# Attention with mixed heads and a gated feed-forward: moving four of a group's six products with v inside and across units

## The chip, the cores and the metric

The kernel runs on one core of a Trainium2 chip. The metric is the device time of one execution in microseconds. "Before" was timed in three runs, and one further execution was profiled.

## What is computed

For 4 batches, 12 heads, 448 positions and head size 64, scores are mixed over the heads before and after the softmax; the result, laid out as 1792 tokens of width 768, goes through a bilinear feed-forward of width 1536. The random inputs q, k and w_pre are multiplied by 8.

```python
scores = scale * np.matmul(q, k.transpose(0, 1, 3, 2))
scores = np.einsum('bhij,hg->bgij', scores, w_pre)
scores = scores - np.max(scores, axis=-1, keepdims=True)
attn = np.exp(scores)
attn = attn / (np.sum(attn, axis=-1, keepdims=True) + 1e-09)
attn = np.einsum('bhij,hg->bgij', attn, w_post)
x = np.matmul(attn, v)          # then tokens x (heads * head size)
out = ((x @ w_a) * (x @ w_b)) @ w_out
```

## The kernel before

The attention is cut into 92 units of at most 20 query positions (23 per batch: 6, 6, 6 and 5, from chunks of 120, 120, 120 and 88 positions). The main loop over `s` (L898 to L933) is software-pipelined; one pass does a piece of several units, and the order of the calls in it is the order of the instructions on each engine. TensorE executes in one pass:

- `premix(s)` (L345, tile `mp`): 8 matmul records that mix the heads of the scores of unit `s`, in 60x64 quadrants. `mp` has three buffers of one bank and a unit takes two, so the second block of a unit reuses the buffer of the first block of the unit before it, and waits for that block's exponential.
- one `qk` (L281, tile `pst`): raw scores for a later chunk. `pst` has one buffer (`bufs=1`), so the next `qk` waits until this one is copied out, by VectorE (L306) or by ScalarE (L308). With `OWN = 3` the copy of product `i` of a chunk is ScalarE's where `i % 3 == 0`. From unit 11 to unit 82 there is one `qk` in each unit, with `i = (s + 7) % 6`; from unit 83 on there is none, and pieces of the feed-forward are prepared instead.
- one `av(a, p)` (L429, tile `xp`): the `p`-th of the six products with v of group `a`. It is 16 matmuls that use all 128 rows and 64 columns of the array (128x64). A group is the 6 (or 5) units of one chunk, and its width is 120 (or 88). After the third and the sixth product VectorE copies `xp` out (L438), and a later DMA stores it (L439).
- `postmix(s - 1)` (L391, tile `pp`): 56 matmuls in 60x64 quadrants. It reads the exponentials of unit `s - 1` and `kr` (L373), and it writes two banks that must first have been emptied of unit `s - 2` by `evac_p` (L408, two ScalarE copies).

ScalarE's order in a pass is `evac_p(s - 2)`, two exponentials (L358) each with a read of its sum, and the `pst` copy where it is ScalarE's. VectorE's is two maxima (L355), in 18 units three copies that reorder k (L242 to L244, one set per unit, units 10 to 15, 34 to 39 and 58 to 63), the `pst` copy where it is VectorE's, the `xp` copy if there is one, and three small instructions for the norm (L368, L369, L373).

The products with v stand in the dictionary `items` with the `qk`: L460 to L464 place product `p` of group `a` at unit `u0 + n + AV_AT[p]`, one per unit. A 5-unit group uses `AV_SHORT`, which puts its first two products into one unit. The last group's six products run after the loop. A planner for loads (L466 on) reads only `av_at`, the unit of each product.

```python
    AV_AT = (1, 2, 3, 4, 5, 6)
    AV_SHORT = (2, 2, 3, 4, 5, 6)
            for it in items.get(s, ()):           # qk first, then av
```

Of the kernel before, what the change touches and what calls it, by code (L numbers as in the profile page):

```python
# [22 lines left out]
def talking_heads_bilinear_kernel(  # L23
# [21 lines left out]
    GU = 6  # L45
# [40 lines left out]
    for b in range(B):  # L86
        t0 = 0
        while t0 < S:
            n = min(CHUNK, S - t0)
# [115 lines left out]
    def load_v(b, i):  # L205
        g, i = divmod(i, V_PIECES // 2)
        to, of = vt[b % 2][g], v[b, g]
        if i < 3:
            heads = slice(2 * i, 2 * i + 2)
            nc.sync.dma_start(out=to[:C, heads], in_=of[:C, heads])  # L210
        elif i < 5:
            heads = slice(3 * (i - 3), 3 * (i - 3) + 3)
            nc.sync.dma_start(out=to[C:P, heads, :R - 1], in_=of[C:, heads, :R - 1])
        elif i == 5:
            for j in range(R - 1):
                nc.sync.dma_start(out=to[P:, :, j], in_=of[C + Y * j:C + Y * j + Y, :, R - 1])
        else:
            nc.sync.dma_start(out=to[C:, :, R - 1], in_=of[:C, :, R - 1])
# [91 lines left out]
    def halves(n):  # L310
        return [(o, min(QH, n - o)) for o in range(0, n, QH)]

    def gather(u):
        c, o, n = units[u]
        sbt[u] = [sb_p.tile([128, S], F32, tag=f"sb{e}", name="sb") for e in range(2)]
        for i, (t, m) in enumerate(halves(n)):
            r = 64 * (i // 2)
            nb = chunks[c][2] // QB
            k_ = (o + t) // QB
            r0 = 64 * (t % QB // QH)  # L320
            if k_ < nb:
                rows = st[c][r0:r0 + QH * nb].rearrange("(i k) h s -> k i h s", k=nb)[k_]
            else:
                rows = st[c][r0 + QH * nb:r0 + QH * nb + m]
            (nc.sync if ALONE <= u <= AH and i % 2 else nc.gpsimd).dma_start(out=sbt[u][i % 2][r:r + m * H], in_=rows)  # L325

    def blocks_of(u):
        n = units[u][2]
        return [(u, j, min(QB, n - QB * j)) for j in range(2) if n > QB * j]
# [4 lines left out]
    def premix(u):  # L334
        n = units[u][2]
        tiles = sbt.pop(u)
        for k_ in blocks_of(u):
            mt[k_[:2]] = ps.tile([128, 512], F32, tag="m", name="mp", bufs=3)[:, :S]
        for i in (0, 2, 1, 3):
            if i >= len(halves(n)):  # L340
                continue
            m = halves(n)[i][1] * H
            r, col = 64 * (i // 2), 64 * (i % 2)
            M = 64 if n == QU or i == 0 else m
            nc.tensor.matmul(mt[u, i // 2][col:col + M], lhsT=wp[r:r + m, :M], rhs=tiles[i % 2][r:r + m])  # L345

    def smax(k_):
        u, j, n = k_
        m = rows_of(n)
        mp = mt.pop((u, j))  # L350
        if j == 0:
            rss[u] = w_p.tile([128, 2], F32, tag="rs", name="rs", bufs=12)
        nm = w_p.tile([128, 1], F32, tag="nm", name="nm", bufs=16)
        a = w_p.tile([128, S], F32, tag="an", name="a", bufs=AB)
        nc.vector.tensor_reduce(nm[:m], mp[:m], axis=AXX, op=ALU.max, negate=True)  # L355
        if j == 0:
            pace(2 * u, nm)
        nc.scalar.activation(a[:m], mp[:m], ACTF.Exp, bias=nm[:m], scale=1.0, accum_out=rss[u][:m, j:j + 1])  # L358
        at[u, j] = a

    def norm(u):
        rs = rss.pop(u)
        rc = w_p.tile([128, 2], F32, tag="rc", name="rc", bufs=8)
        kr = w_p.tile([128, 2, H * QH], F32, tag="kr", name="kr", bufs=3)
        ms = [rows_of(n) for _, _, n in blocks_of(u)]
        for j0, j1 in ([(0, len(ms))] if ms[0] == ms[-1] else [(0, 1), (1, 2)]):
            m = ms[j0]
            nc.vector.tensor_scalar(rs[:m, j0:j1], rs[:m, j0:j1], 1e-9, None, op0=ALU.add)  # L368
            nc.vector.reciprocal(rc[:m, j0:j1], rs[:m, j0:j1])  # L369
            if j0 == 0:  # L370
                pace(2 * u + 1, rc[:, :1])
            shape = [m, j1 - j0, H * QH]
            nc.vector.tensor_tensor(  # L373
                kr[:m, j0:j1],
                kf[:m].rearrange("p h t -> p (h t)").unsqueeze(1).to_broadcast(shape),
                rc[:m, j0:j1].unsqueeze(2).to_broadcast(shape),
                op=ALU.mult,
            )
        krs[u] = kr.rearrange("p j (h t) -> p j h t", h=H)

    def postmix(u):
        kr = krs.pop(u)
        blocks = blocks_of(u)
        todo = [[(j, r, e) for r in range(R - 1) for e in range(2)] + [(j, R - 1, j)] for j in range(len(blocks))]
        if len(blocks) == 2:
            todo[1] = todo[1][-1:] + todo[1][:-1]
        for j, r, e in [x for t in todo for x in t]:
            x = C * (r + R * e if r < R - 1 else r)
            for i, (_, m) in enumerate(halves(blocks[j][2])):
                rows = slice(64 * i, 64 * i + m * H)  # L390
                nc.tensor.matmul(  # L391
                    pp_t[i][C * e:C * e + C, H * r:H * r + H, j, :m],
                    lhsT=at[u, j][rows, x:x + C],
                    rhs=kr[rows, j, :, :m],
                )
        for j in range(len(blocks)):
            at.pop((u, j))

    def evac_p(u):
        a = group_of[u]  # L400
        n = units[u][2]
        o = (u - groups[a][1]) * QU
        if a not in ptt:
            ptt[a] = big.tile([128, R, H, AVC], F32, tag="pt", name="pt")
        to = ptt[a].rearrange("p r h t -> p (r h) t")
        for i in range(2):
            if n == QU:
                nc.scalar.copy(to[:, :, o + QB * i:o + QB * i + QB], pp_t[i].rearrange("p x j t -> p x (j t)"))  # L408
                continue
            for j, (_, _, m) in enumerate(blocks_of(u)):  # L410
                hs = halves(m)
                if i < len(hs):
                    t0, k = hs[i]
                    t0 += o + QB * j
                    nc.scalar.copy(to[:, :, t0:t0 + k], pp_t[i][:, :, j, :k])
# [23 lines left out]
            later(lambda: nc.sync.dma_start(out=xd[b][:, 3 * g:3 * g + 3, t0:t0 + n], in_=xs[:, :, :n]), 1)  # L439

    items, late, between, after, ready = {}, {}, {}, {}, {}
    starts = [u for u in range(NU) if units[u][1] == 0] + [NU]
    qk_at = {}
    last_prep = starts[NC - 1] - AH - 1
# [12 lines left out]
    av_at = {}  # L457
    for a in range(NA):
        b, u0, n = groups[a]
        for p in range(H // 2):  # L460
            av_at[a, p] = u0 + n + (AV_AT if n == GU else AV_SHORT)[p]
            if a < NA - 1:
                items.setdefault(av_at[a, p], []).append((av, a, p))

    def plan_loads():
        per_b = NC // B  # L466
# [45 lines left out]
    def open_moe():  # L512
        short.close()
        mo["w"] = ctx.enter_context(tc.tile_pool(name="mw", bufs=2))
        mo["x"] = ctx.enter_context(tc.tile_pool(name="mx", bufs=1))
        mo["x"].tile([128, PAD_X], F32, tag="pad", name="pad")
# [335 lines left out]
    with tc.manual_schedule():  # L852
# [45 lines left out]
        for s in range(NU + 2):  # L898
            now[0] = s
            if s == last_prep + 1:  # L900
                open_moe()
            while nxt_g <= min(s + AH, NU - 1) and ready.get(units[nxt_g][0], -1) < s:
                gather(nxt_g)
                nxt_g += 1
            if 0 <= s - V_FIRST < V_PIECES - V_EARLY:
                load_v(0, V_EARLY + s - V_FIRST)
            for fn in todo_at.pop(s, ()):
                fn()
            if s < NU:
                premix(s)  # L910
            if 2 <= s <= NU:
                evac_p(s - 2)
            if s < NU:
                for k_ in blocks_of(s):
                    smax(k_)
            for it in between.get(s, ()):
                it[0](*it[1:])
            for it in items.get(s, ()):
                if it[0] is qk:
                    it += (it[2] % OWN if s not in late else 1,)  # L920
                it[0](*it[1:])
            if s < NU:
                norm(s)
            if 0 <= s - 1 < NU:
                postmix(s - 1)
            for it in late.get(s, ()):
                qk(*it[1:], 0)
            for it in after.get(s, ()):
                it[0](*it[1:])
            for fn in at_end.pop(s, ()):  # L930
                fn()
            if s == NU:
                evac_p(NU - 1)  # L933
# [142 lines left out]
```

## Time and profile before

| what | us |
|---|---|
| median of 3 runs (lowest, highest) | 862.87 (862.2, 865.9) |
| the profiled execution's own time | 862.92 |
| span of the profiled execution, first to last instruction | 861.2 |
| TensorE busy in the span | 837.9 |

In a row of the timeline the columns are the start in us from the start of the span, the duration in us from the first start to the last end, the engine (PE is the matmuls of TensorE, PEld its weight loads, DVE VectorE, ACT ScalarE), the line of the kernel, the operation, output and input tile with their shapes, and the number of instructions merged into the row. In square brackets stands the idle time of the engine before it and what ended that. Matmuls overlap in the array, so the length of a TensorE block is read from its start to the start of the next block.

### The profile page before, as it was taken

How to read it: one execution, taken by the hardware profiler on the slowest of the kernel's cores; microseconds unless marked ns; L12 is line 12 of the kernel's file. 1: busy time of each engine (PE TensorE's matmuls, PEld its weight loads, DVE VectorE, ACT ScalarE, POOL GpSimd, SP SyncE). 2: the span in 40 equal slices, each digit the busy share in tenths (PEclk: the TensorE clock that was granted, in tenths of full speed). 3: DMA queues.
4: the chain of work that ended last, by engine and by line, in shares of the span. 5: the costliest groups of instructions: out<-in, count | busy, mean ns of one | idle time of the engine just before them, and what ended most of it. 6: DMA issues, size and time to landing. Idle time of an engine off the chain costs nothing.

```text
span 861.2 us, 26229 instructions
## 1 busy us (share of the span) xinstructions
PE 837.9 (97%) x10612; PEld 672.9 (78%) x10612; DVE 499.4 (58%) x989; ACT 414.6 (48%) x864; POOL 479.5 (56%) x595
## 2 busy tenths in 40 slices
PE   6999999999999989999999999999999999999998
PEld 3356566566656556799999999999999998999997
DVE  4688677777787767465433433363445244655761
ACT  3577677667777767644323332322233145333330
POOL 6777777677767856036446533678666743222220
PEclk9899999999999999999999999999999999999999
DMA  8777886787979974674543634566565488654551
GB/s 199 177 210 176 188 199 196 181 199 187 205 178 213 202 194 112 194 228 164 190 146 135 217 135 152 193 216 248 198 227 191 151 319 309 216 213 186 200 198 65
DMA packets 105306, 165.90 MB, mean 193 GB/s; under 512 B 50014, under 2 KB 81114, under 8 KB 105186
## 3 DMA queue, kind: packets, MB, share of 16 engines
q1 hardware_dynamic: 76738, 126.11, 46.3%
q0 software_dynamic: 28448, 38.11, 18.6%
q8 instruction: 84, 1.38, 0.7%
q14 instruction: 36, 0.29, 0.1%
HBM read 84.16 MB, written 41.29 MB: 146 GB/s over the span
## 4 chain that ended last, share of the span: by engine, by line
PE 84%; DMA 5%; DVE 3%; issue 2%; POOL 2%; ACT 2%; SPq 1%; DVEq 0%; POOLq 0%; ACTq 0%
PE xp L429 9%; PE pp L391 8%; PE mp L345 7%; PE pst L281 7%; PE pa L639 6%; PE pa L641 6%; PE pb L639 6%; PE pa L640 6%; PE pb L641 6%; PE pb L640 6%; PE po L760 5%; PE po L759 5%; PE po L758 5%; DMA sb<-s 2%; DMA hr<-hd 1%
## 5 line engine op out<-in xcount | busy, mean ns | idle before, releaser
L325 POOL DMA_DIRECT2D sb<-s x354 | 205.2, 592 | 63.8 <-PE mp L345 28.6
L358 ACT ACTIVATE a<-mp,nm 124x448 f32<-124x448 f32 x180 | 112.8, 632 | 58.8 <-DVE nm L355 58.7
L355 DVE TENSOR_REDUCE nm<-mp 124x1 f32<-124x448 f32 x180 | 104.2, 619 | 55.7 <-PE mp L345 55.1
L661 DVE TENSOR_TENSOR hf<-pb,sa 128x448 f32<-128x448 f32 x47 | 29.3, 624 | 164.5 <-PE pb L641 157.7
L429 PEld LDWEIGHTS xp<-pt,v 128*64 128x64 f32 x1536 | 74.1, 136 | 63.5 <-issue 43.5
L645 ACT COPY sa<-pa 128x448 f32<-128x448 f32 x47 | 25.2, 536 | 176.9 <-PE pa L641 176.9
L408 ACT COPY pt<-pp 128x480 f32<-128x480 f32 x176 | 91.3, 576 | 34.0 <-PE pp L391 33.0
L345 PE MATMUL mp<-sb,wp 60*64 60x448 f32 x720 | 98.6, 550 | 4.5 <-DMA sb<-s 2.8
L391 PE MATMUL pp<-kr,a 60*64 60x60 f32 x5040 | 97.6, 222 | 4.8 <-issue 4.2
L640 PE MATMUL pb<-xhl,wh 128*128 128x448 f32 x282 | 102.2, 362 | 0.0
L639 PE MATMUL pb<-xhl,wh 128*128 128x448 f32 x282 | 102.2, 362 | 0.0
L641 PE MATMUL pb<-xhl,wl 128*128 128x448 f32 x282 | 102.2, 362 | 0.0
L391 PEld LDWEIGHTS pp<-kr,a 60*64 60x64 f32 x5040 | 85.1, 134 | 21.4 <-issue 9.6
L281 PE MATMUL pst<-k,q 64*64 64x448 f32 (+1 forms) x728 | 92.7, 545 | 4.6 <-ACT s L308 2.6
L429 PE MATMUL xp<-pt,v 128*64 128x120 f32 (+1 forms) x1536 | 93.4, 265 | 2.4 <-ACT a L358 0.8
L641 PE MATMUL pa<-xhl,wl 128*128 128x448 f32 x264 | 95.7, 362 | 0.0
L639 PE MATMUL pa<-xhl,wh 128*128 128x448 f32 x264 | 95.7, 362 | 0.0
L640 PE MATMUL pa<-xhl,wh 128*128 128x448 f32 x264 | 95.7, 362 | 0.0
L630 POOL TENSOR_TENSOR wl<-v,wh 128x768 fp32r<-128x768 f32 x21 | 38.9, 1851 | 98.6 <-ACT wh L629 98.6
L760 PE MATMUL po<-hhl,wl 128*128 128x448 f32 x252 | 91.5, 363 | 0.8 <-POOL wl L630 0.8
L758 PE MATMUL po<-hhl,wh 128*128 128x448 f32 x252 | 91.3, 362 | 0.0
L759 PE MATMUL po<-hhl,wh 128*128 128x448 f32 x252 | 91.3, 362 | 0.0
(117 smaller groups left out, 1430.3 us busy)
## 6 DMA issues: line engine op xcount, KB each, us to landing
sb<-s POOLq DMA_DIRECT2D x350, 105.0 KB, 5.0
hhl<-hd SPq DMA_DIRECT2D x42, 448.0 KB
v<-in_w_ab_dram SPq DMA_DIRECT2D x22, 768.0 KB
hd<-hf SPq DMA_DIRECT2D x48, 224.0 KB
v<-in_w_out_dram SPq DMA_DIRECT2D x12, 768.0 KB
wod<-cw SPq DMA_DIRECT2D x21, 384.0 KB
v<-wod SPq DMA_DIRECT2D x21, 384.0 KB
xhl<-xd SPq DMA_DIRECT2D x24, 224.0 KB
```

What stands on the lines that cost most here:

```text
L281: nc.tensor.matmul(out[64 * e:64 * e + cols.stop - cols.start], lhsT=qt[c, i // QG][rows, i % QG, cols], rhs=kt[b, i][rows],)
L325: (nc.sync if ALONE <= u <= AH and i % 2 else nc.gpsimd).dma_start(out=sbt[u][i % 2][r:r + m * H], in_=rows)
L345: nc.tensor.matmul(mt[u, i // 2][col:col + M], lhsT=wp[r:r + m, :M], rhs=tiles[i % 2][r:r + m])
L358: nc.scalar.activation(a[:m], mp[:m], ACTF.Exp, bias=nm[:m], scale=1.0, accum_out=rss[u][:m, j:j + 1])
L391: nc.tensor.matmul(pp_t[i][C * e:C * e + C, H * r:H * r + H, j, :m], lhsT=at[u, j][rows, x:x + C], rhs=kr[rows, j, :, :m],)
L429: nc.tensor.matmul(xp[64 * e:64 * e + 64, p % 3, :n], lhsT=vt[b % 2][g][:, h % G, r], rhs=ptt[a][:, r, h, :n], start=(r == 0), stop=(r == ...
L639: nc.tensor.matmul(o, lhsT=hh[:, off + k], rhs=x[:, 0, k], start=first, stop=False)
L640: nc.tensor.matmul(o, lhsT=hh[:, off + k], rhs=x[:, 1, k], start=False, stop=False)
L641: nc.tensor.matmul(o, lhsT=ll[:, off + k], rhs=x[:, 0, k], start=False, stop=last)
L758: nc.tensor.matmul(po, lhsT=hh[:, k], rhs=t[:, 0, k], start=(k == 0), stop=False)
L759: nc.tensor.matmul(po, lhsT=hh[:, k], rhs=t[:, 1, k], start=False, stop=False)
L760: nc.tensor.matmul(po, lhsT=ll[:, k], rhs=t[:, 0, k], start=False, stop=(k == KH2 - 1))
```

## The change

For a group of 6 units the second product with v (`p` = 1) leaves its place between `qk` and `postmix` and comes behind `postmix` in the same pass; the third (`p` = 2) comes ahead of `premix` in its pass, which is the next one. The fifth and the sixth go the same way. So in TensorE's order products 2 and 3 stand next to each other across the boundary of two passes, as do 5 and 6. The first and the fourth stay. In the 5-unit groups only the fifth and the sixth move. The unit of each product is unchanged. The `xp` copy after the third and the sixth product moves with them, ahead of the maxima of its pass; its store (one pass later) and all loads keep their places.

```diff
     items, late, between, after, ready = {}, {}, {}, {}, {}
+    ahead, behind = {}, {}
+    AV_WHEN = (items, behind, ahead) * 2
...
             if a < NA - 1:
-                items.setdefault(av_at[a, p], []).append((av, a, p))
+                when = AV_WHEN[p] if n == GU or p > 2 else items
+                when.setdefault(av_at[a, p], []).append((av, a, p))
...
             for fn in todo_at.pop(s, ()):
                 fn()
+            for it in ahead.get(s, ()):
+                it[0](*it[1:])
             if s < NU:
                 premix(s)
...
             if 0 <= s - 1 < NU:
                 postmix(s - 1)
+            for it in behind.get(s, ()):
+                it[0](*it[1:])
             for it in late.get(s, ()):
```

## Rows read from the trace of the kernel before

**Rows 1.** The page: busy time of the engines; the chain that ended last.

```profile
PE 837.9 (97%) x10612; PEld 672.9 (78%) x10612; DVE 499.4 (58%) x989; ACT 414.6 (48%) x864; POOL 479.5 (56%) x595
...
PE 84%; DMA 5%; DVE 3%; issue 2%; POOL 2%; ACT 2%; SPq 1%; DVEq 0%; POOLq 0%; ACTq 0%
```

**Rows 2.** Timeline of TensorE's matmuls, unit 32 and the start of unit 33.

```profile
137.91 0.94 PE L345 MATMUL mp<-sb,wp 60*64 60x448 f32 x8
138.66 0.93 PE L281 MATMUL pst<-k,q 64*64 64x448 f32 x8
139.53 1.04 PE L429 MATMUL xp<-pt,v 128*64 128x120 f32 x16
140.50 1.04 PE L391 MATMUL pp<-kr,a 60*64 60x60 f32 x56
141.36 0.94 PE L345 MATMUL mp<-sb,wp 60*64 60x448 f32 x8
```

**Rows 3.** Timeline of TensorE's matmuls, a unit with two products and one with one.

```profile
113.95 1.44 PE L429 MATMUL xp<-pt,v 128*64 128x88 f32 x32
115.32 1.04 PE L391 MATMUL pp<-kr,a 60*64 60x60 f32 x56
...
117.80 0.83 PE L429 MATMUL xp<-pt,v 128*64 128x88 f32 x16
118.56 0.63 PE L391 MATMUL pp<-kr,a 60*64 60x60 f32 x28
```

**Rows 4.** Timeline of TensorE's matmuls, early units that have no product with v.

```profile
28.15 0.98 PE L281 MATMUL pst<-k,q 64*64 64x448 f32 x8
28.95 0.99 PE L391 MATMUL pp<-kr,a 60*64 60x60 f32 x56
29.77 1.36 PE L345 MATMUL mp<-sb,wp 60*64 60x448 f32 x8
31.01 0.98 PE L281 MATMUL pst<-k,q 64*64 64x448 f32 x8
...
34.22 0.98 PE L281 MATMUL pst<-k,q 64*64 64x448 f32 x8 [0.44 <-ACT s L308]
```

**Rows 5.** Timeline of TensorE's matmuls near the end, a `postmix` before a product.

```profile
356.55 1.04 PE L391 MATMUL pp<-kr,a 60*64 60x60 f32 x56
357.52 1.04 PE L429 MATMUL xp<-pt,v 128*64 128x120 f32 x16
```

**Rows 6.** Timeline of ScalarE and of the weight loads around those early units.

```profile
29.37 0.63 ACT L358 ACTIVATE a<-mp,nm 124x448 f32<-124x448 f32 x1 [2.47 <-DVE nm L355]
...
30.15 0.20 PEld L345 LDWEIGHTS mp<-sb,wp 60*64 60x64 f32 x6 [0.24 <-ACT a L358]
...
33.27 0.90 ACT L308 COPY s<-pst 124x896 f32<-124x896 f32 x1
```

**Rows 7.** Timeline of ScalarE in unit 32, where the `pst` copy is ScalarE's.

```profile
139.67 0.63 ACT L358 ACTIVATE a<-mp,nm 124x448 f32<-124x448 f32 x1 [0.50 <-DVE nm L355]
...
140.90 0.90 ACT L308 COPY s<-pst 107x896 f32<-107x896 f32 x1
```

**Rows 8.** Timeline of a unit whose `pst` copy is VectorE's: its `premix`, maxima, copy.

```profile
215.75 0.94 PE L345 MATMUL mp<-sb,wp 60*64 60x448 f32 x8
...
216.78 1.16 DVE L355 TENSOR_REDUCE nm<-mp 124x1 f32<-124x448 f32 x2 [1.12 <-PE mp L345]
217.86 1.08 DVE L306 COPY s<-pst 107x896 f32<-107x896 f32 x1
```

**Rows 9.** Timeline of unit 12, which reorders k: its `premix` and its `pst` copy.

```profile
66.28 0.94 PE L345 MATMUL mp<-sb,wp 60*64 60x448 f32 x8
...
68.86 1.08 DVE L306 COPY s<-pst 124x896 f32<-124x896 f32 x1
```

**Rows 10.** Timeline of ScalarE in the last units: two `evac_p`.

```profile
347.64 1.04 ACT L408 COPY pt<-pp 128x480 f32<-128x480 f32 x2
...
357.64 1.03 ACT L408 COPY pt<-pp 128x480 f32<-128x480 f32 x2 [0.47 <-PE pp L391]
```

## The prediction

> **What bounds it now.** I read the page first: TensorE is busy 97% of the span and carries 84% of the chain that ended last [rows 1]. So a unit costs what TensorE's blocks cost, and the next view is the timeline of its matmuls in a unit, each block from its start to the start of the next: `premix` 0.75, `qk` 0.87, product with v 0.97, `postmix` 0.86, together 3.45 us [rows 2]. Nothing idles between them. Then I read the two engines that empty TensorE's banks in the same unit, to see how far behind `premix` each bank is free again: that tells what a shorter distance between two blocks would run into.
>
> **What TensorE itself saves.** The change removes no instruction and adds none; it puts two products side by side. That unit pair has a precedent, the unit where a 5-unit group runs two products: 32 matmuls take 1.37, 16 take 0.76 [rows 3], so the second costs 0.61, that is 0.15 less. Of width 120 two then take 0.97 + 0.82 = 1.79. Next, `qk` directly before `postmix`, as in the early units, takes 0.80 instead of 0.87, and the `postmix` behind it 0.82 instead of 0.86 [rows 2, 4]. Against that, a `postmix` directly before a product takes 0.97 where it took 0.86 [rows 2, 5]: 0.11 more, so 0.93 for one that follows `qk`. A product directly before `premix` is nowhere to be seen; by the nearest row it costs `premix` nothing, and the outer bound is the 0.11 just read.
>
> Take three successive units: E (product at its end), F (product at its front), M (product in the middle). Before: 3 x 3.45 = 10.35. After, TensorE alone: F 0.75 + 0.80 + 0.82, M 0.75 + 0.87 + 0.97 + 0.86, E 0.75 + 0.80 + 0.93, and 1.79 for the pair, sum 10.09. That is **0.26 saved for each pair**. There are 12 six-unit groups with two pairs and 3 five-unit groups with one, 27 pairs, so 7.0 us if nothing waits.
>
> The drop is the price of leaving and entering the 128x64 shape twice instead of once. The Trainium skill ("TensorEngine Tiling", Tiling Modes) says that a change of tiling mode drains TensorE; rows 3 agree with it, and by that rule alone the time would be 855.9 us. The same page (Performance Considerations, PSUM Bottleneck) says that tiling quickens TensorE but not the emptying of PSUM, which speaks against the change.
>
> **What then waits.** The products also served as cover. Between the `qk` of F and that of M there now stand only a `postmix` and a `premix`, and before the change there was a product too. Counting from F's `premix`, TensorE would reach M's `qk` at 0.75 + 0.80 + 0.82 + 0.75 = 3.12. Three things must be done by then:
>
> (a) M's second `mp` block needs F's first exponential. That ends 139.67 + 0.63 - 137.91 = 2.39 after `premix` [rows 2, 7]. The early units show the wait: exponential over at 30.00, weights loaded at 30.15, next block at 31.01 [rows 4, 6]. So 0.15 later the loads go on, and 0.75 (unhindered) to 0.86 (that row) later `qk` starts; I take 0.80. M's `qk` starts at 3.34, a wait of 0.22 (0.17 to 0.28).
>
> (b) `pst` must be empty. VectorE's copy follows its maxima and ends 217.86 + 1.08 - 215.75 = 3.19 after `premix` [rows 8]; `qk` follows a copy by 0.05 (33.27 + 0.90 to 34.22) [rows 4, 6], 3.24. That is less than (a), so the wait stays 0.22. Where VectorE reorders k first, the copy ends at 68.86 + 1.08 - 66.28 = 3.66 [rows 9], and the wait is 3.71 - 3.12 = 0.59.
>
> (c) Where the copy is ScalarE's it comes behind both exponentials and ends 140.90 + 0.90 - 137.91 = 3.89 [rows 2, 7]; the wait is 3.94 - 3.12 = **0.82**.
>
> None of these shows before, since the product's 0.97 lay over them. Which case a pair meets follows from `i = (s + 7) % 6` at F. In batch 1, and for the 5-unit group of batch 0, F's copy is ScalarE's: 7 pairs of kind (c). In batches 0, 2 and 3 it is VectorE's: 16 pairs, of which units 12, 15, 58 and 61 also reorder k. The last 4 pairs (units 84, 87, 90, 93) have no `qk`.
>
> Two smaller waits. ScalarE's late copy pushes the next `evac_p` (1.04 [rows 10]) to 3.89 + 1.04 = 4.93, and a first product of the next group in M, due at 3.94 + 0.87 = 4.81, needs it: 0.17 more, 4 times. In batch 2 and unit 52 it is M's copy that is ScalarE's; it ends late for the `evac_p` that E's `postmix` needs, which now has no product before it. Exponentials of M to about 5.7, copy to 6.63, `evac_p` to 7.66, against 7.57 at which `postmix` is due: about 0.13, 7 times.
>
> The moved `xp` copy runs on VectorE while `premix` runs and before its maxima can start, 1.03 after `premix` [rows 8], so I cost it at nothing; without that cover its half microsecond would delay the maxima. Its store on SP's queue, the gathers on POOL's and all loads keep their pass, so no queue is reordered.
>
> **The last four pairs.** There the units have no `qk`, and `evac_p` is nearer the path. At unit 89 `postmix` would be due near 347.9, but `evac_p` ends at 347.64 + 1.04 = 348.68 [rows 10]: 0.8 lost, 0.3 regained, +0.5. At unit 92 it would be due at 357.5 and `evac_p` ends at 358.67: 1.2 lost, some 0.5 of it regained or lost already, +0.7. Units 84 and 87 already wait for ScalarE in every unit; I put +0.8 for both. Sum +2.0, between 0 and 4.
>
> **The sum.**
> - 7 plain pairs of VectorE (batches 0 and 3, unit 75): 7 x (0.22 - 0.26) = -0.3.
> - 5 plain pairs with the late `evac_p`: 5 x (0.22 + 0.13 - 0.26) = +0.45.
> - 4 pairs with k: 4 x (0.59 - 0.26) + 2 x 0.13 = +1.6.
> - 7 pairs of ScalarE: 7 x (0.82 - 0.26) + 4 x 0.17 = +4.6.
> - last 4: +2.0.
>
> Total +8.3, on the profiled execution's own 862.92 (0.05 above the median of the runs): **871.2**, which I give as 871. At the lower ends (waits 0.05 shorter, last pairs free) it is about +4 or 867; with every wait 0.15 longer and the last pairs at 4, about +14 or 877.
>
> **Rivals.** About 0.5% (4.3 us) is what a measurement of this kernel can tell from no change.
>
> *Nothing waits, faster:* the pairs keep their 0.26 and the time is 862.9 - 7.0 = 855.9. It needs F's `pst` empty and its exponential done by 3.12 after `premix`. For it: VectorE's copy misses that by only 0.12 and the exponential's wait is 0.2. Against it: ScalarE's copy misses it by 0.8, and rows 4 show such waits as soon as a product is absent. It decides at whether M's `premix` and `qk` begin 2.37 and 3.12 after F's. Chance 0.10.
>
> *A draw:* the waits on VectorE's side turn out hidden and only the 7 of ScalarE remain: 20 x (-0.26) + 7 x (0.99 - 0.26) = -0.1, so about 863. For it: 0.22 is a small number built from three rows. Against: rows 6 show the wait for the exponential directly. Chance 0.20.
>
> *No saving, only waits, slower still:* if entering 128x64 from `postmix` and leaving it into `premix` cost what leaving and entering cost now (0.11 at both ends), the saving falls to 0.15 or less and each late bank makes the next late: 27 x 0.11 = 3 more, 874, and 880 with delays that carry over. Chance 0.10. That the order on TensorE doesn't change can be left out: rows 2 and 3 follow the order of the calls.
>
> **How the numbers follow.** My forecast has 0.60, with 866 to 877 as its own range. Faster by over 0.5% (below 858.6) is the first rival, 0.10. Within 0.5% is the draw and the low edge of the forecast, 0.22. Slower by over 0.5% (above 867.2) is the rest, 0.68. The range 862 to 877 holds the forecast, the draw and the milder half of the last rival; out stay the first rival and the worst of the last.
>
> **What would show it.** In the trace after: products of 32 matmuls in one row of about 1.8 us, 27 pairs where there were 3 double rows of the 5-unit groups. The `postmix` of F behind `qk` by 0.80. In F to M, a `qk` of M that starts 3.9 after F's `premix` in batch 1, with ScalarE's copy (L308) as the releaser, and about 3.3 in batches 0 and 2, with weight loads of `premix` that wait for an exponential (L358). Three units E, F, M should take about 10.3 in batch 0 and 10.9 in batch 1. Batch 1 alone should be some 4 us longer than before, batch 0 about as long. If batch 1's units are no longer than batch 0's, (c) is wrong; if all units are shorter by 0.26 a pair, the first rival is right.

## The result and the profile after

The changed kernel takes 868.91 us (median of 22 runs) beside 863.31 for the kernel before (22 runs); the ratio is 1.0062, interval 1.0041 to 1.0084. That is slower by 3.5 to 7.3 us. The ratio leaves out two runs of the changed kernel that are over 1.5% above its fastest. The profiled execution took 866.28, its span 864.6; it is 3.4 us longer than the profiled execution of the kernel before (862.92), so the pair of traces shows less than the runs.

The page, lines of busy time and of the chain that ended last:

```profile
PE 836.8 (97%) x10612; PEld 684.1 (79%) x10612; DVE 498.7 (58%) x989; ACT 410.2 (47%) x864; POOL 478.0 (55%) x595
...
PE 79%; DMA 8%; ACT 4%; DVE 4%; issue 2%; POOL 2%; SPq 1%; DVEq 0%; ACTq 0%; POOLq 0%
```

Against [rows 1] TensorE's share of the chain fell from 84% to 79%, while ScalarE's rose from 2% to 4% and VectorE's from 3% to 4%: steps on other engines have come into the chain. DMA's share rose too, from 5% to 8%; the long transfers in it lie at other places in each of the two traces, and no run follows them up. TensorE's busy time, 836.8 against 837.9, hides this, since a block of matmuls that is held half way through counts as busy to its end (1.19 for 0.94 below).

TensorE's matmuls in batch 0, unit 9 (front, F), unit 10 (middle, M), unit 11 (end, E) and the start of unit 12:

```profile
55.95 0.98 PE L345 MATMUL mp<-sb,wp 60*64 60x448 f32 x8
56.75 0.93 PE L281 MATMUL pst<-k,q 64*64 64x448 f32 x8
57.50 0.99 PE L391 MATMUL pp<-kr,a 60*64 60x60 f32 x56
58.32 1.19 PE L345 MATMUL mp<-sb,wp 60*64 60x448 f32 x8
...
59.24 1.02 PE L281 MATMUL pst<-k,q 64*64 64x448 f32 x8
60.19 1.04 PE L429 MATMUL xp<-pt,v 128*64 128x120 f32 x16
61.16 1.04 PE L391 MATMUL pp<-kr,a 60*64 60x60 f32 x56
62.02 0.94 PE L345 MATMUL mp<-sb,wp 60*64 60x448 f32 x8
62.78 0.93 PE L281 MATMUL pst<-k,q 64*64 64x448 f32 x8
63.53 0.99 PE L391 MATMUL pp<-kr,a 60*64 60x60 f32 x56
64.45 1.86 PE L429 MATMUL xp<-pt,v 128*64 128x120 f32 x32
66.25 0.98 PE L345 MATMUL mp<-sb,wp 60*64 60x448 f32 x8
```

Read from start to start: the pair takes 1.80, `premix` behind it 0.80, `qk` before `postmix` 0.75, `postmix` before the pair 0.92. The `premix` at 58.32 lasts 1.19 where an unhindered one lasts 0.94: it was held inside. Three units take 66.25 - 55.95 = 10.30 where three of [rows 2] take 10.35.

What the `qk` at 59.24 waited for, in VectorE's row and in that of the weight loads:

```profile
58.10 1.08 DVE L306 COPY s<-pst 107x896 f32<-107x896 f32 x1
...
59.24 0.23 PEld L281 LDWEIGHTS pst<-k,q 64*64 64x64 f32 x8 [0.51 <-DVE s L306]
```

The copy of `pst` ends at 58.10 + 1.08 = 59.18, and the weights of `qk` are loaded 0.06 later.

ScalarE and TensorE in batch 1, units 32 (F) and 33 (M), where F's copy of `pst` is ScalarE's:

```profile
140.23 0.98 PE L345 MATMUL mp<-sb,wp 60*64 60x448 f32 x8
141.03 0.93 PE L281 MATMUL pst<-k,q 64*64 64x448 f32 x8
141.79 0.99 PE L391 MATMUL pp<-kr,a 60*64 60x60 f32 x56
142.60 1.19 PE L345 MATMUL mp<-sb,wp 60*64 60x448 f32 x8
144.22 0.98 PE L281 MATMUL pst<-k,q 64*64 64x448 f32 x8 [0.43 <-ACT s L308]
...
142.03 0.64 ACT L358 ACTIVATE a<-mp,nm 124x448 f32<-124x448 f32 x1 [2.01 <-DVE nm L355]
...
143.27 0.90 ACT L308 COPY s<-pst 107x896 f32<-107x896 f32 x1
144.05 1.05 ACT L408 COPY pt<-pp 128x480 f32<-128x480 f32 x2
...
151.19 0.98 PE L345 MATMUL mp<-sb,wp 60*64 60x448 f32 x8
```

The copy ends at 143.27 + 0.90 = 144.17, and `qk` starts at 144.22, 3.99 after F's `premix`. It is the wait that [rows 7] could not show, because a product lay over it. Three units take 151.19 - 140.23 = 10.96. The bracket's 0.43 is less than the loss, since the `premix` ahead of it was late too and its last matmuls are modelled to end at 143.79.

TensorE in unit 12, where k is reordered, and M behind it; then the `premix` of unit 83, the `postmix` calls of units 86 and 92 (both E), and the first product of the feed-forward behind the attention:

```profile
66.25 0.98 PE L345 MATMUL mp<-sb,wp 60*64 60x448 f32 x8
...
70.01 0.98 PE L281 MATMUL pst<-k,q 64*64 64x448 f32 x8 [0.21 <-DVE s L306]
...
323.38 0.94 PE L345 MATMUL mp<-sb,wp 60*64 60x448 f32 x8
...
335.87 1.50 PE L391 MATMUL pp<-kr,a 60*64 60x60 f32 x56 [0.56 <-ACT pt L408]
...
361.09 1.11 PE L391 MATMUL pp<-kr,a 60*64 60x60 f32 x28 [0.67 <-ACT pt L408]
...
369.71 0.47 PE L642 MATMUL pa<-xhl,wa 128*128 128x448 f32 x1
```

Behind unit 12 `qk` starts 3.76 after F's `premix`. In the last stage `postmix` of E waits for `evac_p` (L408) where a product stood before it. From the `premix` of unit 83 to that first product it is 369.71 - 323.38 = 46.33 us; before it was 43.39, by these two rows of the kernel before:

```profile
322.71 0.94 PE L345 MATMUL mp<-sb,wp 60*64 60x448 f32 x8
...
366.10 0.48 PE L639 MATMUL pa<-xhl,wa 128*128 128x448 f32 x1
```

The `premix` of unit 28 and that of unit 51, between which the seven pairs with ScalarE's copy in F lie, in the kernel before and then in the change:

```profile
123.61 0.94 PE L345 MATMUL mp<-sb,wp 60*64 60x448 f32 x8
...
205.32 0.94 PE L345 MATMUL mp<-sb,wp 60*64 60x448 f32 x8
```

```profile
123.77 0.94 PE L345 MATMUL mp<-sb,wp 60*64 60x448 f32 x8
...
208.30 0.94 PE L345 MATMUL mp<-sb,wp 60*64 60x448 f32 x8
```

That is 81.71 and 84.53 us, 2.8 more, where seven times the 0.60 that units 32 to 34 lost would be 4.2.

### The profile page after: what moved, and what is told of

Read it like the earlier page. It is cut to its first block, busy times and chain, and to the rows that moved or that the text cites. A ratio compares the mean times of both kernels' runs of the same rounds, so it can differ in the third digit from the quotient of the medians.

```text
span 864.6 us, 26221 instructions
## 1 busy us (share of the span) xinstructions
PE 836.8 (97%) x10612; PEld 684.1 (79%) x10612; DVE 498.7 (58%) x989; ACT 410.2 (47%) x864; POOL 478.0 (55%) x595
## 4 chain that ended last, share of the span: by engine, by line
PE 79%; DMA 8%; ACT 4%; DVE 4%; issue 2%; POOL 2%; SPq 1%; DVEq 0%; ACTq 0%; POOLq 0%
PE xp L429 8%; PE pp L391 6%; PE pa L642 6%; PE pb L644 6%; PE pb L643 6%; PE pb L642 6%; PE pa L644 6%; PE pa L643 6%; PE pst L281 6%; PE mp L345 6%; PE po L763 5%; PE po L761 5%; PE po L762 5%; DMA sb<-s 2%; ACT a L358 2%
## 5 line engine op out<-in xcount | busy, mean ns | idle before, releaser
L391 PEld LDWEIGHTS pp<-kr,a 60*64 60x64 f32 x5040 | 93.7, 135 | 38.4 <-issue 22.4
L345 PE MATMUL mp<-sb,wp 60*64 60x448 f32 x720 | 100.9, 553 | 4.4 <-DMA sb<-s 2.7
L281 PE MATMUL pst<-k,q 64*64 64x448 f32 x728 | 91.0, 548 | 9.4 <-ACT s L308 4.6
L408 ACT COPY pt<-pp 128x480 f32<-128x480 f32 x176 | 91.1, 578 | 15.4 <-PE pp L391 14.5
L429 PE MATMUL xp<-pt,v 128*64 128x120 f32 (+1 forms) x1536 | 87.3, 264 | 1.2 <-ACT pt L408 1.0
```

Source lines behind the costliest of these rows:

```text
L281: nc.tensor.matmul(out[64 * e:64 * e + cols.stop - cols.start], lhsT=qt[c, i // QG][rows, i % QG, cols], rhs=kt[b, i][rows],)
L391: nc.tensor.matmul(pp_t[i][C * e:C * e + C, H * r:H * r + H, j, :m], lhsT=at[u, j][rows, x:x + C], rhs=kr[rows, j, :, :m],)
L429: nc.tensor.matmul(xp[64 * e:64 * e + 64, p % 3, :n], lhsT=vt[b % 2][g][:, h % G, r], rhs=ptt[a][:, r, h, :n], start=(r == 0), stop=(r == ...
```

## The experiments

All runs are given as the ratio of their time to that of the kernel before on the same chip, with a 95% interval. All compute the same, except where the text says that a part is left out.

**The copying engine by the unit's place.** If the loss is the wait for ScalarE's copy in F, it goes when VectorE copies in F and ScalarE in E, where the pair of products follows and gives the copy time.

```diff
-                    it += (it[2] % OWN if s not in late else 1,)
+                    it += (0 if s in behind else 1 if s in ahead or s - 1 in ahead else it[2] % OWN if s not in late else 1,)
```

> The change whole, but the engine that copies pst is chosen by the unit's place: ScalarE in the unit with the product at its end, VectorE in the front unit and in the one after it. Theory (the wait for ScalarE's copy in the front unit is the main loss): in batch 1 three units fall from 10.96 us to about 10.3, M's qk starts 3.3 after F's premix (3.8 where k is reordered, units 35 and 38), and the late evac_p of batch 2 goes; some 4 to 5 us less than the change as it was, so about the time of before (ratio 0.998 to 1.004), the last units still some 3 us longer than before. Rival (the loss lies in the last units or in shape switches): no more than 1 us less than the change as it was, ratio about 1.006.

Measured: 1.0022 (0.9993 to 1.0050). The same three units of batch 1:

```profile
143.41 0.98 PE L345 MATMUL mp<-sb,wp 60*64 60x448 f32 x8
...
146.71 1.02 PE L281 MATMUL pst<-k,q 64*64 64x448 f32 x8
...
153.72 0.98 PE L345 MATMUL mp<-sb,wp 60*64 60x448 f32 x8
```

`qk` starts 3.30 after `premix` and three units take 10.31, not 10.96. No product was moved back; with the copy changed the ratio fell by 0.0040 of 0.0062. The two intervals touch (1.0041 to 1.0050), so the units show the cause more firmly than the totals do.

**Without the 7 pairs of ScalarE, and only these.** In the first their products stay in the middle, in the second (without the `not`) all others do.

```diff
-                when = AV_WHEN[p] if n == GU or p > 2 else items
+                front = av_at[a, p] + (p % 3 == 1)
+                pair = (n == GU or p > 2) and not (front <= 82 and front % 3 == 2)
+                when = AV_WHEN[p] if pair else items
```

> The change without the 7 pairs whose front unit has ScalarE's copy of pst (batch 1 and unit 29); their products stay in the middle. Theory: batch 1 goes back to 10.36 us for three units, 7 x 0.6 = 4 us less than the change as it was, ratio to before 1.001 to 1.004. Rival (all pairs cost alike): 27 pairs cost 5.6 us together, so 7 of them give back 1.5 us, ratio about 1.005.

> Only those 7 pairs are moved. Theory: each costs 0.6 us, together 4 us over before, ratio 1.004 to 1.006, three units of batch 1 take 10.96 us. Rival (all pairs cost alike): 1.5 us over before, ratio 1.002.

Measured: 1.0039 (1.0018 to 1.0060) without them, 1.0028 (1.0001 to 1.0054) with them alone; the two together, 0.0067, are the whole change's 0.0062. The 7 alone came out below the 1.004 to 1.006 that was expected. By time alone neither rival is excluded: 1.005 lies in the first interval and 1.002 in the second. For the units the trace decides: with the 7 alone, F's `premix` stands at 139.42, M's `qk` at 143.41 and the next F's `premix` at 150.38, 10.96 for three units. For the total it does not: from unit 28 to unit 51 this trace takes 83.77, 2.1 over the kernel before and not 4.2.

```profile
139.42 0.98 PE L345 MATMUL mp<-sb,wp 60*64 60x448 f32 x8
...
143.41 0.98 PE L281 MATMUL pst<-k,q 64*64 64x448 f32 x8 [0.44 <-ACT s L308]
...
150.38 0.98 PE L345 MATMUL mp<-sb,wp 60*64 60x448 f32 x8
```

**Only the last four pairs** (`pair = (n == GU or p > 2) and front > 82`).

> Only the last four pairs are moved (units 84, 87, 90, 93, where no qk stands). Theory: 2 to 3 us over before, ratio 1.002 to 1.0035, the time from unit 83's premix to the first pa product is 46.3 us instead of 43.4, with postmix waiting for evac_p in units 83, 86, 89 and 92. Rival (these units wait for VectorE and ScalarE anyway, so nothing is lost): ratio within 0.001 of 1, 43.4 us.

Measured: 1.0013 (0.9993 to 1.0033), too little to tell by time. In the trace the stretch takes 366.56 - 320.85 = 45.71, 2.3 more than before, and `postmix` of unit 86 waits 0.56 for `evac_p`, as in the whole change. The loss is there in the trace; the 1.002 that was expected lies inside the interval, and so does 1.000.

**The wait in every pair.** The edit of the first experiment with the engines exchanged: 0 for `s in ahead`, 1 for `s in behind`.

> The change whole, with the suspected wait put into every pair: ScalarE copies pst in all front units, VectorE in the two others. Theory: M's qk starts 4.0 after F's premix everywhere, three units take 10.95 us in batches 0 and 2 as well; 16 more pairs pay 0.2 to 0.7 us each, some 9 us over the change as it was, ratio to before 1.014 to 1.019. Rival (the choice of the copying engine does not matter, the loss lies elsewhere): ratio as for the change, 1.006.

Measured: 1.0151 (1.0103 to 1.0200). Unit 9, free of this wait in the change as it was, and the next F:

```profile
56.27 0.98 PE L345 MATMUL mp<-sb,wp 60*64 60x448 f32 x8
...
60.26 0.98 PE L281 MATMUL pst<-k,q 64*64 64x448 f32 x8 [0.43 <-ACT s L308]
...
67.22 0.98 PE L345 MATMUL mp<-sb,wp 60*64 60x448 f32 x8
...
373.43 0.47 PE L642 MATMUL pa<-xhl,wa 128*128 128x448 f32 x1
```

3.99 again, and 10.95 for three units: more of the suspected cause gave more of the loss. That the total came out as the working said is in part luck. Its span, 872.6, is 11.4 over that of the kernel before, but 4.1 of this lie behind the last row, in the feed-forward, which no edit touches (872.6 - 373.43 = 499.2 against 861.2 - 366.10 = 495.1). The stretch from unit 11 to unit 83 took 264.39, in the change 261.36: 3 us more and not 9.

**Only the 12 plain pairs, and the best by the theory.** The first moves pairs only where F's copy is VectorE's, k is not reordered and a `qk` stands; the second chooses the copying engine by place and moves 17 pairs.

> Only the 12 pairs whose front unit has VectorE's copy, no reordering of k and a qk (batches 0 and 2 with units 75, 78, 81, without 12, 15, 58, 61); copies as before. Theory: each trades 0.30 us saved on TensorE for a wait of 0.2 and in batch 2 for a late evac_p besides, so nothing that can be told from before, ratio 0.998 to 1.001; three units of batch 0 take 10.3 us. Rival (a pair costs by itself, whatever copies pst): 12 of 27 pairs cost 2.5 us, ratio 1.003.

> The copies by place as in e1_roles, and pairs only where neither k is reordered nor qk is missing: 17 pairs. Theory: 17 x 0.07 us saved, about 1 us less than before, ratio 0.997 to 1.000, which is at the edge of what can be told. Rival (nothing waits once ScalarE's copy is out of the front unit, so 17 x 0.30 is saved): 5 us less than before, ratio 0.994.

Measured: 1.0002 (0.9975 to 1.0029) and 1.0003 (0.9973 to 1.0032). Neither beats the kernel before; the second's rival, 0.994, is excluded, and the first's, 1.003, by a hair. A plain pair is worth next to nothing, and that is what 0.29 saved and about 0.23 waited should give (three units take 10.30, and 10.07 without any wait, as the next runs show).

**Is the saving real?** Here a part is left out: the softmax's maximum is taken over 224 of 448 columns. That shortens VectorE's first work, so the first exponential and the copy come earlier. With the copies by place and the 23 pairs that have a `qk`; and the kernel before with the same cut.

```diff
-        nc.vector.tensor_reduce(nm[:m], mp[:m], axis=AXX, op=ALU.max, negate=True)
+        nc.vector.tensor_reduce(nm[:m], mp[:m, :S // 2], axis=AXX, op=ALU.max, negate=True)
```

> The softmax's maximum is taken over the first 224 of 448 columns (the other half is left out), which halves VectorE's first work in a unit; the copies go by place as in e1_roles, and the 23 pairs with a qk are moved. Theory (the saving of 0.30 us a pair is real and only the waits for the exponential and for VectorE's copy eat it): the first exponential and the copy come 0.25 and 0.5 us earlier, the waits go, three units take 10.05 to 10.1 us, and the time is 5 to 7 us under that of e9_half_max_before, ratio to before 0.992 to 0.995. Rival (two products side by side save nothing that lasts, or M waits for something else): no difference from e9_half_max_before.

> The kernel before with the maximum over the first 224 of 448 columns only. Theory (TensorE sets the unit, VectorE's maxima are covered): three units still take 10.36 us, ratio 0.998 to 1.001. Rival (VectorE or the softmax chain holds the units back already): three units take less than 10.3 us, ratio below 0.996.

Measured: 0.9950 (0.9920 to 0.9981) and 0.9966 (0.9939 to 0.9993). The expectation that the cut alone does nothing failed a little in the total, though its units hold: premixes at 54.07 and 64.43, 10.36. Part of it is the last stage: from unit 83's `premix` to the feed-forward it takes 42.52 with the cut, 43.39 without. Of the pair kernel:

```profile
54.40 0.98 PE L345 MATMUL mp<-sb,wp 60*64 60x448 f32 x8
...
56.77 0.96 PE L345 MATMUL mp<-sb,wp 60*64 60x448 f32 x8
57.53 0.95 PE L281 MATMUL pst<-k,q 64*64 64x448 f32 x8
...
64.47 0.98 PE L345 MATMUL mp<-sb,wp 60*64 60x448 f32 x8
```

M's `premix` lasts 0.96 instead of 1.19, `qk` starts 3.13 after F's `premix`, and three units take 10.07: the 0.29 is there as soon as nothing waits. The totals differed by 0.0016 only, which is within the noise, so both were run again, with a third kernel that keeps the cut but lets ScalarE copy in F, as in the change.

> The kernel of e8_half_max_pairs once more, for a second profile and a second set of times beside e12_before_again. Theory (the 0.29 us a pair reaches the total, and the first comparison was blurred by the waits for nothing shown, 11.9 us of them in that profile): ratio to before lower than that of e12_before_again by 0.005 to 0.008. Rival (about as much comes back as waits for nothing shown inside postmix): lower by 0.003 or less, with more of those waits than in e12_before_again.

> The kernel of e9_half_max_before once more, as the partner of e11_pairs_again. Theory: ratio 0.997 to 1.000, three units 10.36 us.

> The maximum over 224 columns, the 23 pairs with a qk, and the copies as in the change (ScalarE's in the front unit of 7 pairs). Theory: the 7 pairs still wait, but 0.25 us less, as ScalarE starts earlier: M's qk 3.7 after F's premix, three units of batch 1 10.65 us; the other pairs as in e11_pairs_again. So some 4 us over e11_pairs_again, ratio 0.996 to 1.000. Rival (with VectorE's work cut all waits go): as e11_pairs_again.

Measured: 0.9914 (0.9882 to 0.9946), 0.9973 (0.9943 to 1.0003) and 0.9980 (0.9948 to 1.0011). This time the pairs are 0.0059 ahead of their partner, within the 0.005 to 0.008 expected; the first time it was 0.0016. The means of the two sets, 0.9932 and 0.9970, are 0.0038 or 3.2 us apart, about half of 23 x 0.29 = 6.7 us. With ScalarE's copy in F none of it is left (0.9980 beside 0.9973); M's `qk` in batch 1 then starts 142.82 - 139.06 = 3.76 after `premix`, and three units take 10.72:

```profile
139.06 0.98 PE L345 MATMUL mp<-sb,wp 60*64 60x448 f32 x8
...
142.82 0.98 PE L281 MATMUL pst<-k,q 64*64 64x448 f32 x8 [0.44 <-ACT s L308]
```

## Why the prediction was right, and where a term was off

The sign, the range and the cause held: 0.26 saved in a pair, and a wait that a product had covered taking its place. The forecast was +8.3 us, 871; measured were +5.4 (3.5 to 7.3) and 868.91. That the number came so near is partly luck, as the terms show.

- *What TensorE saves.* Foretold 0.26, found 0.29 (10.07 for three units with no wait, against 10.36). `qk` before `postmix` takes 0.75, not 0.80: the early rows [rows 4] from which it was taken were a little long. `premix` behind a product, which no row showed, pays 0.05 (0.80 for 0.75), between the bounds of 0 and 0.11.
- *(a) and (b), VectorE's pairs.* M's `qk` was put at 3.34 and stands at 3.29 (55.95 to 59.24); with k 3.71 foretold, 3.76 found. The near hit hides a wrong choice: (a), the exponential, was taken to end last, and in this unit it is (b), VectorE's copy, 0.06 before `qk`. The exponential does hold `premix` inside, but from its end (57.75 + 0.63 = 58.38) to `qk` it is 0.86 where the forecast had 0.95. In batch 2 `qk` stands at 3.38 behind the same copy; the profile names no cause for the rest. A plain pair was foretold to give 0.04 and gives 0.05 in batch 0 (10.35 to 10.30). The runs with only such pairs show no difference.
- *(c), ScalarE's pairs.* 3.94 foretold, 3.99 found; 10.9 for three units, 10.96 found. Taken away, put into all pairs and softened, this wait moved the units each time as worked out. By the units it is the largest term, 7 x 0.60 = 4.2; the runs do not show it to be the largest part of the loss, since the seven pairs alone cost 0.0028 (2.4 us) and the rest without them 0.0039 (3.4 us).
- *The 0.17 of `evac_p` behind (c).* This term was wrong. Unit 36 has a first product; its `qk` starts at 155.18 and the product at 156.10, 0.92 later, as in unit 33, which has no such product (144.22 to 145.13, 0.91). The `evac_p` of [rows 10] was put at 4.93 after `premix`; in batch 1 it ends at 144.05 + 1.05 - 140.23 = 4.87, when the product is due. Four times 0.17 fall away, 0.7 us.
- *The 0.13 of `evac_p` in batch 2.* It is not there in every pair. With F in unit 52, E's `postmix` follows its `qk` by 0.76, as elsewhere. With F in unit 55 `postmix` takes 231.88 - 230.49 = 1.39 instead of 0.92, because a piece of the feed-forward's preparation (L559) stands ahead of `evac_p` on ScalarE. The forecast had no such piece in it:

```profile
229.36 0.58 ACT L559 ACTIVATE cvm<-cvm 128x384 f32<-128x384 f32 x1
229.82 1.04 ACT L408 COPY pt<-pp 128x480 f32<-128x480 f32 x2
...
230.49 1.46 PE L391 MATMUL pp<-kr,a 60*64 60x60 f32 x56
231.88 1.86 PE L429 MATMUL xp<-pt,v 128*64 128x120 f32 x32
```

- *The last four pairs.* Foretold 2.0, in the trace 2.9 with the whole change and 2.3 alone. So 2.9 of the 3.4 us between the two profiled executions lie here.
- *The rest.* Without the 0.17 and with the last pairs at 2.9 the terms give 8.5, and the runs 5.4. So two wrong terms cancel, and about 3 us came back elsewhere. The traces show a part of it: from unit 28 to unit 51 the terms make 4.2 and the stretch lost 2.8. The sign that batch 1 alone would be some 4 us longer is therefore met only in part (units 23 to 45: 85.62 against 82.81). From unit 11 to unit 83 the whole loss is 1.3 (260.10 to 261.36), though every kind of pair shows its wait. In the same stretch waits of another kind shrank from 6.6 to 4.1 us (below).

The first rival needed M's `qk` at 3.12; it came at 3.29 or later in every kind of pair, and only with VectorE's maxima cut to half at 3.13. The draw needed VectorE's waits hidden; the held `premix` (1.19 for 0.94) shows them. The third rival put leaving and entering at 0.11 each; leaving costs 0.05.

The Trainium skill ("TensorEngine Tiling", Tiling Modes) has it that a change of tiling mode drains TensorE; the 0.29 that comes back with one visit less to the 128x64 shape agrees. The same page of the Trainium skill (Performance Considerations, PSUM Bottleneck) has it that tiling speeds up TensorE but not the emptying of PSUM. Here the order and not the tiling made TensorE faster, and the trace agrees that the emptying did not follow: `pst` was copied out 3.23 (VectorE) to 3.94 us (ScalarE) after F's `premix`, where TensorE could be back at 3.13.

## What to carry to other kernels

A block on the bounding engine may also be cover: before it is moved away from between two users of a single buffer, add up from the moment the first user's input is ready to the moment the buffer is free again, and compare that with the engine's own work that is left between them. Here TensorE would have been back at the buffer after 3.1 us where the other engines needed 3.2 to 3.9, and the gain of 0.3 was gone. Which engine frees the buffer was worth 0.66 us in three units (10.96 against 10.30), the order of the matmuls 0.05; but the best choice of both did not beat the kernel before.

## What was not expected

TensorE has waits for which the views of the profile name no cause ("issue"), mostly inside `postmix`, at other places in each profile. Between 50 and 330 us they came to 6.6 us in the kernel before. In the kernels with 7 or more waits of full length for ScalarE's copy they were less: 4.1 (the change), 3.5 (the 7 pairs alone), 3.1 (all pairs); in those without, 6.3 to 11.9. The kernel with 7 shorter waits for ScalarE had 8.7, and each number is one profile.

The traces do show what these waits go with. They hold the time of every DMA packet, and one queue carries instructions:

```profile
q8 instruction: 84, 1.38, 0.7%
```

Its packets are 16384 bytes each, about 5.2 us apart between 50 and 330 us, and between two of them TensorE starts some 256 matmuls and weight loads. Over the 14 profiles, 74 of the 75 issue waits of 0.5 us or more in that stretch end 1.25 to 1.95 us after such a packet has landed, and the last one 1.96 us after; a moment taken at random would do so in about one case of seven. So TensorE most likely waits there for its own instructions, which arrive late. This would also be how some 3 us came back: while TensorE waits for a bank, the next instructions can arrive. No run changed the loading of instructions, so that part is argued and not shown.

These waits also blur the totals: 11.9 and 10.2 us of them in the first pair of runs with the halved maximum, 9.3 and 6.6 in the second. And they are not the only blur. In two profiles, that with the wait in every pair and the first of the pairs with the halved maximum, the feed-forward took 499.2 and 499.7 us from its first product to the end of the span, in the other twelve 494.7 to 495.5. In its last product the matmuls follow each other every 0.21 us instead of 0.20, at a granted clock of 1.00 in both cases. The cause stays open, and 4 us of the totals of these two runs may be due to it.
